# The start of a fused attention and gated-MLP block on one core: the first unit's scores by pairs of heads, and the loads and turns around them in another order

## The chip, the core and the metric

The kernel runs on one core of one Trainium2 chip. The metric is the device time of one execution in microseconds. A core has five engines with a queue each: TensorE (PE in the profile; its weight loads are shown as PEld), VectorE (DVE), ScalarE (ACT), GpSimd (POOL) and SyncE (SP, which here only issues DMAs). An engine works through its queue in order, and each instruction waits there for what it needs from others.

## What is computed

An adaLN block: six modulation vectors from `c`, grouped-query attention with 32 query heads on 8 cached key and value heads, then a gated MLP with a spatial product. Cut to what matters:

```python
mod = (silu(c) @ w_mod).reshape(1, 6, 1, 512)      # sa, ca, ga, sb, cb, gb
h = layernorm(x) * (1 + ca) + sa                   # x: 1 x 2048 x 512, bfloat16
q = (h @ wq)                                       # 32 heads of 128
k, v = repeat(k_cache, 4), repeat(v_cache, 4)      # 8 heads x 2048 x 128
p = softmax(q @ k.T * 128 ** -0.5)
x = x + ga * ((p @ v) @ wo)
h = layernorm(x) * (1 + cb) + sb
z = gelu(h @ w_in)                                 # 2 x 896
g = w_sp @ layernorm(z[..., 896:]) + b_sp          # along the sequence
x = x + gb * ((z[..., :896] * g) @ w_out)
```

## The kernel before

The 2048 rows of x are 16 tiles of 128 rows, in 4 chunks of 4 tiles. The attention works in 128 units: unit u is key/value group g = u // 16 and row tile j = u % 16, with the 4 query heads of that group. A unit has 8 slots. In a slot `qk` (L992) makes two tiles of 128 keys against the 4 heads (two matmuls of 512 columns into one of two buffers `s_ps`, L1026), and ScalarE takes the exponential of those 1024 columns into `pT` (L1033). One unit later `pv` (L1074) multiplies by v, eight matmuls of 129 columns a slot (L1082); later still `wo_proj` (L1106) adds the output projection. From unit 8 on every second unit is done by rows in another way (L1003 to L1023). The loop at L1375 writes all this out by hand, unit by unit and slot by slot: in each slot first what the table `later` holds for it (entered by `at`), then the scores, then a share of `pv`, then what the table `fill` holds, mostly the projection of q for a coming chunk (`qproj`, L935), a matmul or two a slot. Nothing reorders it: the order of the calls is the order in each engine's queue.

Before unit 0 can start, a chain has to run once, and the change is in it:

- Loads. SyncE's queue takes, in this order: the first 1024 columns of the modulation weight (`wmod_a`, two halves by columns, L707), the first group's `wq` (two halves along the contraction, L752), half of the first 8 key tiles (`k_nat`, L753), x tile 1, the other half, x tiles 2 and 3 (L756), the last 8 key tiles transposed by DMA (L760), v (L732), the rest of x (L764) and wo. ScalarE's queue takes `c` (L703) and then x tile 0 (L704).
- Modulation. VectorE and ScalarE make silu(c) (L773 to L782). `mod_part` (L853) multiplies a part of the weight by it, 16 matmuls of one column a part; `mod_copy` (L865) copies the two results to `modc`, adding 1 to the scale.
- x tile 0. VectorE takes statistics (`ln_stats`, L696), GpSimd the reciprocal root (`rstd_of`, L676), VectorE normalises (L687), TensorE transposes in four pieces (L894), and VectorE and ScalarE apply the modulation to two pieces each, which gives `hT` (L816 and L908).
- q of tile 0 for all 4 heads: 16 matmuls of 128 columns (L921) into two banks, with the turn of key tiles 0 to 3 (`k_turn`, L872) between; then VectorE and ScalarE copy a bank each (L929).
- `warm` (L784) puts matmuls on zeros into TensorE's queue, here and there, that nobody reads.

Inside unit 0, slot 0's fill `first_norm` (L1198) turns key tiles 4 to 7, and takes statistics and normalises tiles 1 to 3; `first_turn` in slot 3 turns tile 1 to hT (`ln1_turn`, L825: transposes on TensorE, modulation on VectorE), slot 6 turns tiles 2 and 3. Slots 4 and 5 project q of tile 1, slot 7 and unit 1 q of tiles 2 and 3 (`rest_q`, L1216). Chunk 1 of x is handled by `ln1_at` (L1221): its statistics stand in unit 0, slot 7, its normalisation in unit 1, slot 2, its transposes by DMA from SyncE one slot later (`ln1_dma`), its modulation (`ln1_dma_mod`) in unit 2, slot 2. Chunk 2 follows from unit 2, slot 4. GpSimd's queue loads the other 2 MB of the modulation weight in unit 2, slot 5 (`wmod_b` in the tile `wsp`, L1231); 32 matmuls on it stand in unit 4, slot 4 (`mod_cols_b`, L1171).

Of the kernel before, what the change touches and what calls it, by code (L numbers as in the profile page):

```python
# [12 lines left out]
ACT = mybir.ActivationFunctionType  # L13
ALU = mybir.AluOpType
AX = mybir.AxisListType
P = 128
# [559 lines left out]
def kernel(  # L576
# [19 lines left out]
    nc = tc.nc  # L596
# [103 lines left out]


    c_bf = res.tile([P, NDT], BF16, name="c_bf")
    nc.scalar.dma_start(out=c_bf[:], in_=c_dram)  # L703
    nc.scalar.dma_start(out=x_sb[:, 0, :], in_=x_dram[:, 0, :])  # L704
    for i in range(2):
        part = slice(i * D, (i + 1) * D)
        nc.sync.dma_start(out=wmod_a[:, :, part], in_=wmod_dram[:, :, part])  # L707
    k_nat = early.tile([P, SK], BF16, name="kT")

    def load_k_nat(half):  # L710
        t0, t1 = half * NKT // 4, (half + 1) * NKT // 4
# [85 lines left out]
    def ln1_stats(j0, n):  # L797
        for j in range(j0, j0 + n):
            ln_stats(mv1, j, x_sb[:, j, :])
        return rstd_of(mv1[:, j0 : j0 + n, :], n, "ln1")  # L800

    def ln1_norm(j0, n, rstd):
        xns = []
        for j in range(j0, j0 + n):
            xn = res.tile([P, D], BF16, name="xn1", bufs=4)
            normalise(xn[:], x_sb[:, j, :], mv1[:, j, 0:1], rstd[:, j - j0 : j - j0 + 1])
            xns.append(xn)
        return xns
# [73 lines left out]
            copy(out=kT0[:, part[0] * P : (part[-1] + 1) * P], in_=k_ps[:, 0 : n * P])  # L882


    xns0 = ln1_norm(0, 1, ln1_stats(0, 1))
    mc_ps = bank("misc")
    warm(10)
    mod_part(0, wmod_a, 0, mc_ps)
    warm(6)
    mod_part(1, wmod_a, D, mc_ps)  # L890

    x_ps = [bank("misc")[:].bitcast(BF16), bank2()[:, 0:512].bitcast(BF16)]
    for dt in range(NDT):
# [2 lines left out]
            xns0[0][:, dt * P : (dt + 1) * P],  # L896
            ident[:],
        )
    mod_copy(0, mc_ps)
    warm(2)  # L900
    hT_of(0)
    for k in range(2):
        for dt in (2 * k, 2 * k + 1):
# [9 lines left out]
                    bias=modc[:, dt : dt + 1],  # L913
                )
    qTs = {0: early.tile([P, REP, 512], BF16, name="qT")}
    q_ps = [bank("misc"), bank2()]
    for dt in range(NDT):
        if dt == 2:
            k_turn((0, 1, 2, 3), (nc.vector.tensor_copy, nc.scalar.copy))
        for hh in range(REP):  # L920
            nc.tensor.matmul(  # L921
                q_ps[hh // 2][:, hh % 2 * P : (hh % 2 + 1) * P],
                lhsT=wqs[0][:, dt, hh * DH : (hh + 1) * DH],
                rhs=hTs[0][:, dt, 0:P],
                start=(dt == 0 and hh % 2 == 0),
                stop=(dt == NDT - 1 and hh % 2 == 1),
            )
    for hf, copy in enumerate((nc.vector.tensor_copy, nc.scalar.copy)):
        copy(  # L929
            out=qTs[0][:, 2 * hf : 2 * hf + 2, 0:P],  # L930
            in_=q_ps[hf][:, 0 : 2 * P].rearrange("p (h q) -> p h q", h=2),
        )
    warm(2)

    def qproj(b, heads, c0, n, banks=("misc", "misc")):  # L935

# [55 lines left out]
    def qk(u, i):  # L992
# [10 lines left out]
        if by_rows(u):  # L1003
            hh, half = divmod(i, 2)
            for c in range(2):
                k0 = (2 * half + c) * 512
                nc.tensor.matmul(  # L1007
                    s_ps[:, c * 512 : (c + 1) * 512],
                    lhsT=qTs[b][:, hh, jj * P : (jj + 1) * P],
                    rhs=groups[g]["kT"][:, k0 : k0 + 512],  # L1010
                    start=True,
                    stop=True,
                )
            nc.scalar.activation(  # L1014
                out=rows_of(u, hh)[:, half * HK : (half + 1) * HK],
                in_=s_ps[:],
                func=ACT.Exp,
                scale=inv_sqrt_dh,
                accum_out=rsums[u][:, i : i + 1],
            )  # L1020
            if half == 1:
                at(*divmod(u * NSLOT + i + 2, NSLOT), lambda: turn_rows(u, hh))
            return  # L1023
        for h in range(2):
            kt = 2 * i + h
# [564 lines left out]
```

## Time and profile before

| | us |
|---|---|
| median of 3 runs | 1311.34 (1311.04 to 1311.53) |
| the profiled execution | 1311.72 |
| its span, first to last instruction | 1309.7 |
| TensorE busy in the span | 1301.9 (99%) |
| ScalarE busy | 1112.4 (85%) |
| VectorE busy | 684.2 (52%) |
| GpSimd busy | 58.7 (4%) |

The 2.0 us between the span and the execution lie around the span and hold no instruction of the program. Matmuls are pipelined, so a busy TensorE may be one at less than its peak.

Where the start goes (stretches of the span; busy us of each engine):

| stretch | what | TensorE | VectorE | ScalarE |
|---|---|---|---|---|
| 0 to 11.26 | to the first exponential of unit 0 | 9.80 | 4.79 | 3.04 |
| 11.26 to 18.36 | unit 0 | 6.72 | 6.21 | 6.85 |
| 18.36 to 26.75 | unit 1 | 8.39 | 6.05 | 7.91 |
| 26.75 to 48.20 | units 2 to unit 4, slot 3 | 21.45 | 11.23 | 19.23 |

A line of the timeline gives start, us, engine, line, operation, what it writes and reads, count, and in brackets the idle time of the engine before it and what ended that. An exponential of 1024 columns is 1.02 long, but the next one starts 0.91 after it.

### The profile page before, as it was taken

Reading aid. Unit: us, or ns where it says so; the run is one execution under the profiler, and the core shown is the slowest. Engines: PE = TensorE matmul, PEld = TensorE weight load, DVE = VectorE, ACT = ScalarE, POOL = GpSimd, SP = SyncE. Lnnn points to the kernel's source line nnn. Section 1 sums busy time; section 2 is a strip of 40 time slices with the busy share of each in tenths; the row PEclk is TensorE's granted clock in tenths of the full one; section 3 lists DMA queues with packets and bytes.
Section 4 is the critical chain, followed back from the end, with each engine's and each line's share of the span. In section 5 each row is a group of like instructions: output and inputs, shape, how many; then the busy total and the mean of one; then the engine's idle time right before and its main releaser. Section 6 shows DMA issues by size and latency. Waiting matters only on the chain.

```text
span 1309.7 us, 24370 instructions
## 1 busy us (share of the span) xinstructions
PE 1301.9 (99%) x9527; PEld 736.3 (56%) x9527; DVE 684.2 (52%) x1693; ACT 1112.4 (85%) x1533; POOL 58.7 (4%) x116
## 2 busy tenths in 40 slices
PE   9999999999999999999999999999999999999998
PEld 5665555555555555555555555555555555644445
DVE  6544544444445454444454544444555588784443
ACT  7899999999999999999999999999999999550000
POOL 1200000000000000000000000000000011120000
PEclk9999999999999999999999999999999999999999
DMA  7668778877887677867986678678776688464300
GB/s 181 153 94 154 129 127 159 154 126 133 153 168 143 126 139 155 145 130 137 169 160 127 125 156 156 128 137 153 163 144 124 119 141 147 105 134 96 85 21 31
DMA packets 607723, 174.45 MB, mean 133 GB/s; under 512 B 597264, under 2 KB 603664, under 8 KB 607600
## 3 DMA queue, kind: packets, MB, share of 16 engines
q1 hardware_dynamic: 600576, 153.67, 65.0%
q0 software_dynamic: 4432, 16.91, 4.2%
q10 hardware_dynamic: 2592, 2.23, 0.5%
q8 instruction: 77, 1.26, 0.4%
q14 instruction: 46, 0.38, 0.1%
HBM read 21.89 MB, written 2.10 MB: 18 GB/s over the span
## 4 chain that ended last, share of the span: by engine, by line
PE 97%; DMA 2%; DVE 1%; POOL 0%; issue 0%; ACT 0%; SPq 0%; DVEq 0%
PE o_ps L1082 18%; PE s_ps L1026 18%; PE s_ps L1007 16%; PE o_ps L1061 16%; PE misc L1114 8%; PE misc L947 8%; PE misc L1457 7%; PE s_ps L1292 2%; PE s_ps L1331 2%; PE o_ps L1490 1%; DMA wsp<-in_w_mod_dram 1%; PE s_ps L1490 0%; DMA wmod_a<-in_w_mod_dram 0%; DMA hT<-xn 0%; DVE hT L816 0%; DVE bnst L698 0%
## 5 line engine op out<-in xcount | busy, mean ns | idle before, releaser
L1033 ACT ACTIVATE pT<-s_ps 128x1024 bf16<-128x1024 f32 x552 | 560.4, 1024 | 32.1 <-PE s_ps L1026 10.1
L1082 PEld LDWEIGHTS <-pT 128*128 128x128 bf16 x4416 | 295.3, 98 | 128.9
L1082 PE MATMUL o_ps<-v,pT 128*128 128x129 bf16 x4416 | 339.7, 220 | 0.0
L1026 PE MATMUL s_ps<-qT,kT 128*128 128x512 bf16 x1104 | 328.1, 379 | 0.3 <-ACT pT L1033 0.2
L1007 PE MATMUL s_ps<-kT,qT 128*128 128x512 bf16 x944 | 280.7, 379 | 0.1
L1014 ACT ACTIVATE win_sb<-s_ps 128x1024 bf16<-128x1024 f32 x238 | 243.4, 1024 | 3.5
L1114 PE MATMUL misc<-wo_g,oT 128*128 128x512 bf16 x512 | 194.0, 379 | 0.0
L947 PE MATMUL misc<-hT,wq_g 128*128 128x512 bf16 (+2 forms) x520 | 187.0, 371 | 0.1
L1026 PEld LDWEIGHTS <-kT 128*128 128x128 bf16 x1104 | 107.2, 98 | 115.0 <-issue 2.3
L1014 ACT ACTIVATE pn<-s_ps 128x1024 bf16<-128x1024 f32 x156 | 159.4, 1023 | 2.0 <-ACT wmod_a L1014 0.3
L1061 PEld LDWEIGHTS <-v 128*128 128x128 bf16 x944 | 92.3, 98 | 111.5
L958 DVE CAST qT<-misc 128x512 bf16<-128x512 f32 x125 | 85.6, 685 | 123.5 <-PE misc L947 123.5
L1070 DVE CAST oT<-o_ps 128x512 bf16<-128x512 f32 x59 | 40.8, 691 | 195.0 <-PE o_ps L1061 195.0
L1061 PE MATMUL o_ps<-wsp,v 128*128 128x512 bf16 x480 | 142.1, 379 | 0.0
L1061 PE MATMUL o_ps<-pT,v 128*128 128x512 bf16 x464 | 138.0, 379 | 0.0
L1007 PEld LDWEIGHTS <-qT 128*128 128x128 bf16 x944 | 92.2, 98 | 61.7 <-issue 0.2
L1047 DVE TENSOR_TENSOR tot<-rs 128x1 f32<-128x1 f32 x236 | 36.1, 153 | 127.3 <-ACT win_sb L1014 84.9
L1457 PE MATMUL misc<-wsp,z 128*128 128x512 bf16 (+2 forms) x560 | 100.5, 336 | 0.0
L1052 DVE TENSOR_SCALAR win_sb<-win_sb,rall 128x2048 bf16<-128x2048 bf16 x119 | 89.6, 753 | 4.4 <-DVE rall L1050 0.3
L1014 ACT ACTIVATE wmod_a<-s_ps 128x1024 bf16<-128x1024 f32 x78 | 79.8, 1023 | 0.0
L1457 PEld LDWEIGHTS <-z 128*128 128x128 bf16 x560 | 50.5, 98 | 48.4 <-issue 0.2
L1127 DVE TENSOR_TENSOR xacc<-misc,xacc 128x512 f32<-128x512 f32 x112 | 76.0, 679 | 0.0
(111 smaller groups left out, 817.4 us busy)
## 6 DMA issues: line engine op xcount, KB each, us to landing
v<-in_A_v_cache_dram POOLq DMA_DIRECT2D x7, 512.0 KB, 6.6
wq_g<-in_A_wq_dram POOLq DMA_DIRECT2D x7, 512.0 KB, 4.9
wo_g<-in_A_wo_dram POOLq DMA_DIRECT2D x7, 512.0 KB, 4.3
wsp<-in_w_mod_dram POOLq DMA_DIRECT2D x1, 2048.0 KB, 11.8
out_dram<-yout ACTq DMA_DIRECT2D x16, 128.0 KB, 1.7
win_sb<-in_B_w_in_dram POOLq DMA_DIRECT2D x1, 1792.0 KB, 8.1
x_sb<-in_A_x_dram SPq DMA_DIRECT2D x3, 512.0 KB, 8.1
oT<-onorm SPq DMA_TRANSPOSE x69, 2.8
```

What stands on the lines that cost most here:

```text
L947: nc.tensor.matmul(ps[0][:, o0 : o0 + n], lhsT=wqs[g][:, dt, hh * DH : (hh + 1) * DH], rhs=hTs[ch][:, dt, c0 : c0 + n], start=(dt == 0), s ...
L958: nc.vector.tensor_copy(out=dst, in_=src)
L1007: nc.tensor.matmul(s_ps[:, c * 512 : (c + 1) * 512], lhsT=qTs[b][:, hh, jj * P : (jj + 1) * P], rhs=groups[g]["kT"][:, k0 : k0 + 512], sta ...
L1014: nc.scalar.activation(out=rows_of(u, hh)[:, half * HK : (half + 1) * HK], in_=s_ps[:], func=ACT.Exp, scale=inv_sqrt_dh, accum_out=rsums[u ...
L1026: nc.tensor.matmul(s_ps[:, h * 512 : (h + 1) * 512].rearrange("p (r q) -> p r q", r=REP), lhsT=groups[g]["kT"][:, kt * P : (kt + 1) * P], ...
L1033: nc.scalar.activation(out=pTs[u][:, 2 * i : 2 * i + 2, :], in_=s_ps[:].rearrange("p (k q) -> p k q", k=2), func=ACT.Exp, scale=inv_sqrt_dh,)
L1052: nc.vector.tensor_scalar(out=rows, in0=rows, scalar1=rinv, scalar2=None, op0=ALU.mult)
L1061: nc.tensor.matmul(o_pss[u][:], lhsT=groups[g]["v1"][:, kt, 0:DH], rhs=pTs[u][:, kt, :], start=(kt == 0), stop=(kt == NKT - 1),)
L1082: nc.tensor.matmul(o_ps[:, hh % 2, 0 : DH + 1], lhsT=pTs[u][:, kt, hh * P : (hh + 1) * P], rhs=groups[g]["v1"][:, kt, 0 : DH + 1], start=( ...
L1114: nc.tensor.matmul(X_ps[:], lhsT=oTs[u][:, hh, :], rhs=groups[g]["wo"][:, hh, :], start=(hh == 0), stop=(hh == REP - 1),)
L1127: nc.vector.tensor_tensor(out=xaccs[j][:], in0=X_ps[:], in1=xaccs[j][:], op=ALU.add)
L1457: nc.tensor.matmul(g_pss[f][:, :n], lhsT=z2[:, st, f * P : (f + 1) * P], rhs=wsp[t][:, st, c0 : c0 + n], start=(st == 0), stop=(st == NT - ...
```

## The change

- On ScalarE's queue x tile 0 is issued ahead of `c`.
- `wmod_a` is loaded in a piece of three quarters of the contraction and one of the last quarter, with all 1024 columns each, instead of two pieces by columns. Its matmuls go with it: `mod_first` takes one of four parts of the contraction, 8 matmuls, and accumulates all 8 columns in one bank; the 1 of the scale is added by a matmul of a constant into the same bank, so that one copy replaces `mod_copy`. Three parts run before the transposes of x tile 0, the fourth after them and one warm matmul. Six warm matmuls between the parts go, and those around the copy are placed anew.
- The first `wq` is loaded and used by pairs of heads: the first pair's columns, then half of the key tiles, then the second pair's columns. `first_q(0)` projects q for the first pair before unit 0; `first_q(1)` stands in slot 0's fill, behind the scores of slot 0. VectorE copies both. The turn of key tiles 0 to 3 stands behind `first_q(0)`.
- A slot of unit 0 makes four key tiles against two heads instead of two tiles against four: four matmuls of 256 columns. Even slots take the first pair, odd slots the second.
- The turn of tile 1 stands in slot 4 instead of 3, that of tiles 2 and 3 in slot 7 instead of 6, ahead of the statistics of chunk 1; the warm fills and the projection of tile 1 move a slot too. All 16 matmuls of `rest_q` are in unit 1, slots 1 to 6; before, 4 of them were in unit 0, slot 7, and 12 in unit 1, slots 0 to 5.

```diff
     c_bf = res.tile([P, NDT], BF16, name="c_bf")
+    nc.scalar.dma_start(out=x_sb[:, 0, :], in_=x_dram[:, 0, :])
     nc.scalar.dma_start(out=c_bf[:], in_=c_dram)
-    nc.scalar.dma_start(out=x_sb[:, 0, :], in_=x_dram[:, 0, :])
-    for i in range(2):
-        part = slice(i * D, (i + 1) * D)
-        nc.sync.dma_start(out=wmod_a[:, :, part], in_=wmod_dram[:, :, part])
+    for kts in (slice(0, NDT - 1), slice(NDT - 1, NDT)):
+        nc.sync.dma_start(out=wmod_a[:, kts, :], in_=wmod_dram[:, kts, 0 : 2 * D])
...
-    for dts in (slice(0, 2), slice(2, 4)):
-        nc.sync.dma_start(out=wqs[0][:, dts, :], in_=wq_dram[:, dts, 0 : REP * DH])
+    pairs = [slice(2 * hf * DH, 2 * (hf + 1) * DH) for hf in range(2)]
+    nc.sync.dma_start(out=wqs[0][:, :, pairs[0]], in_=wq_dram[:, :, pairs[0]])
     load_k_nat(0)
+    nc.sync.dma_start(out=wqs[0][:, :, pairs[1]], in_=wq_dram[:, :, pairs[1]])
...
+    def mod_first(kt, mc_ps):
+        for col in range(2 * NDT):
+            nc.tensor.matmul(
+                mc_ps[:, col : col + 1],
+                lhsT=wmod_a[:, kt, col * P : (col + 1) * P],
+                rhs=sc_bf[:, kt : kt + 1],
+                start=(kt == 0 and col == 0),
+                stop=(kt == NDT - 1 and col == 2 * NDT - 1),
+            )
+        if kt == 0:
+            nc.tensor.matmul(
+                mc_ps[:, NDT : 2 * NDT],
+                lhsT=mean_bf[:],
+                rhs=ones_bf[:, 0:NDT],
+                start=False,
+                stop=False,
+            )
...
     warm(10)
-    mod_part(0, wmod_a, 0, mc_ps)
-    warm(6)
-    mod_part(1, wmod_a, D, mc_ps)
+    for kt in range(NDT - 1):
+        mod_first(kt, mc_ps)
...
-    mod_copy(0, mc_ps)
-    warm(2)
+    warm(1)
+    mod_first(NDT - 1, mc_ps)
+    nc.vector.tensor_copy(out=modc[:, 0 : 2 * NDT], in_=mc_ps[:, 0 : 2 * NDT])
+    warm(4)
...
-    q_ps = [bank("misc"), bank2()]
-    for dt in range(NDT):
-        if dt == 2:
-            k_turn((0, 1, 2, 3), (nc.vector.tensor_copy, nc.scalar.copy))
-        for hh in range(REP):
...
+    def first_q(hf):
+        q_ps = bank("misc")
+        for dt in range(NDT):
+            for k in range(2):
+                hh = 2 * hf + k
+                nc.tensor.matmul(
+                    q_ps[:, k * P : (k + 1) * P],
+                    lhsT=wqs[0][:, dt, hh * DH : (hh + 1) * DH],
+                    rhs=hTs[0][:, dt, 0:P],
+                    start=(dt == 0 and k == 0),
+                    stop=(dt == NDT - 1 and k == 1),
+                )
+        nc.vector.tensor_copy(
             out=qTs[0][:, 2 * hf : 2 * hf + 2, 0:P],
...
-    warm(2)
+    first_q(0)
+    k_turn((0, 1, 2, 3), (nc.scalar.copy, nc.vector.tensor_copy))
...
-    first = dict(r1=ln1_stats(1, 1))
+    first = {}
...
+        if u == 0:
+            k0, qs = i // 2 * 4, slice(i % 2 * 256, (i % 2 + 1) * 256)
+            for kt in range(4):
+                nc.tensor.matmul(
+                    s_ps[:, kt * 256 : (kt + 1) * 256].rearrange("p (r q) -> p r q", r=2),
+                    lhsT=groups[g]["kT"][:, (k0 + kt) * P : (k0 + kt + 1) * P],
+                    rhs=qTs[b][:, i % 2 * 2 : i % 2 * 2 + 2, 0:P],
...
     def first_norm():
+        first_q(1)
+        first["r1"] = ln1_stats(1, 1)
         k_turn((4, 5, 6, 7), (nc.vector.tensor_copy,))
...
-    at(0, 3, first_turn)
-    at(0, 6, lambda: ln1_turn(2, 2, first["x2"]))
+    at(0, 4, first_turn)
+    at(0, 7, lambda: ln1_turn(2, 2, first["x2"]))
     fill[0, 0] = [first_norm]
-    for i in (1, 2, 3):
+    for i in (2, 3, 4):
         fill[0, i] = [lambda: warm(1)]
     next_q = qproj(0, list(range(REP)), P, P)
-    fill[0, 4], fill[0, 5] = next_q[0:8], next_q[8:16]
+    fill[0, 5], fill[0, 6] = next_q[0:8], next_q[8:16]
     rest_q = qproj(0, [0, 1], 2 * P, 2 * P) + qproj(0, [2, 3], 2 * P, 2 * P)
-    fill[0, 7] = rest_q[0:4]
     for i in range(6):
-        fill[1, i] = rest_q[4 + 2 * i : 6 + 2 * i]
+        fill[1, i + 1] = rest_q[(8 * i + 2) // 3 : (8 * i + 10) // 3]
```

More of the change, by code (lines that the diff above doesn't have):

```diff
@@ L915 @@
     qTs = {0: early.tile([P, REP, 512], BF16, name="qT")}
-    q_ps = [bank("misc"), bank2()]
-    for dt in range(NDT):
-        if dt == 2:
-            k_turn((0, 1, 2, 3), (nc.vector.tensor_copy, nc.scalar.copy))
-        for hh in range(REP):
[L921 to L929, printed above, removed]
+    def first_q(hf):
[11 more added lines that the diff above has]
+        nc.vector.tensor_copy(
             out=qTs[0][:, 2 * hf : 2 * hf + 2, 0:P],
-            in_=q_ps[hf][:, 0 : 2 * P].rearrange("p (h q) -> p h q", h=2),
+            in_=q_ps[:, 0 : 2 * P].rearrange("p (h q) -> p h q", h=2),
         )
-    warm(2)
+    first_q(0)
+    k_turn((0, 1, 2, 3), (nc.scalar.copy, nc.vector.tensor_copy))
     def qproj(b, heads, c0, n, banks=("misc", "misc")):
@@ L1022, in qk @@
                 at(*divmod(u * NSLOT + i + 2, NSLOT), lambda: turn_rows(u, hh))
+            return
+        if u == 0:
[5 more added lines that the diff above has]
+                    rhs=qTs[b][:, i % 2 * 2 : i % 2 * 2 + 2, 0:P],
+                    start=(kt % 2 == 0),
+                    stop=(kt % 2 == 1),
+                )
+            nc.scalar.activation(
+                out=pTs[u][:, k0 : k0 + 4, qs],
+                in_=s_ps[:].rearrange("p (k q) -> p k q", k=4),
+                func=ACT.Exp,
+                scale=inv_sqrt_dh,
+            )
             return
```

## The prediction

> **What bounds the kernel now.** I read the page's first two parts (TensorE is busy 99% of the span, in every slice but the last), then all waits of TensorE, because an engine that is never idle can only be delayed where it waits. There are four in the whole execution (engine, line, what it waited for, total us, times, longest):
>
> ```profile
> PE o_ps L788 <- DVE onorm L769: 1.2, 1, 1.2
> PE misc L857 <- DMA wsp<-in_w_mod_dram: 0.7, 1, 0.7
> PE s_ps L1026 <- ACT pT L1033: 0.2, 1, 0.2
> PE misc L857 <- DMA wmod_a<-in_w_mod_dram: 0.2, 1, 0.2
> ```
>
> Three lie in the first 13 us, which the change rewrites. The second lies behind them, at 48.2 to 48.9 us: TensorE stands 0.69 us for the large part of the modulation weight (it is loaded into the tile wsp). After it TensorE never waits again, so the end moves exactly as far as that point moves. The chain of waits, in order of time (start, us, what), tells what sets it:
>
> ```profile
> 16.93 1.28 DVE hT L816 x4
> 27.29 3.10 DMA hT<-xn
> 30.52 1.38 DVE hT L816 x4
> 36.04 1.00 POOL rstd_ln L683
> 37.04 11.81 DMA wsp<-in_w_mod_dram
> 48.90 0.95 PE misc L857 x32
> ```
>
> The load leaves GpSimd's queue at 37.04, behind the rstd of chunk 2 (L683), which needs chunk 2's statistics, which stand in VectorE's queue behind the modulation of chunk 1 (30.52), which waits for the transposes of chunk 1, which follow its normalisation. The timeline of VectorE shows where that begins:
>
> ```profile
> 16.23 0.69 DVE L958 CAST qT<-misc 128x512 bf16<-128x512 f32 x1 [0.51 <-PE misc L947]
> 16.84 0.72 DVE L816 TENSOR_SCALAR hT<-misc,modc 128x256 bf16<-128x256 bf16 x2
> 17.48 0.72 DVE L816 TENSOR_SCALAR hT<-o_ps,modc 128x256 bf16<-128x256 bf16 x2
> 18.12 0.68 DVE L698 BATCH_NORM_STATS2 bnst<-x_sb 128x6 f32<-128x512 bf16 x1
> ...
> 22.89 1.38 DVE L687 TENSOR_SCALAR xn<-x_sb,mv,rstd_ln 128x512 bf16<-128x512 bf16 x4 [0.91 <-POOL rstd_ln L683]
> ```
>
> No gap stands between 16.23 and the end of chunk 1's statistics: they start at 18.12 because the turn of tiles 2 and 3 (L816, 16.84) is ahead of them. So two clocks run: VectorE's, which lands the load 30.73 us after 18.12, and TensorE's, which arrives at 48.21. The load is the later by 0.69.
>
> **The change, step by step.** Times are those of the profiled execution (span 1309.7, execution 1311.72). M is the start of the modulation's last matmuls, H that of the first hT modulation (8.36 before), S that of unit 0's fourth exponential (13.98 before).
>
> 1. *c behind x tile 0.* Before, c was issued at 0.73, had its first packet at 1.72 and landed at 2.47; x tile 0, second on the queue at 1.14, had its first packet at 2.97 and released VectorE at 4.74. Now c is second. Bounds: 2.95 (its old landing plus the 0.45 that x's issue takes) and 4.70 (x's own landing, though c is 1 KB). I take 3.7: x's first packet, the nearest row, plus the 0.75 from c's first packet to its landing. VectorE waits for c first (L773), and the statistics of x tile 0 are queued behind that wait; x being earlier brings them nothing. The silu was partly hidden: L773 ended at 2.67 and ACT's exponential began only at 2.91, after its table load. Without that, L773 to the statistics is 0.22 + 0.94 (2.91 to 3.85) = 1.16. Statistics at 3.75 + 1.16 = 4.91, xn done 2.34 later (4.74 to 7.08 before): 7.25.
>
> 2. *Weight split along the contraction.* 24 of 32 matmuls and the added 4-column one run after the first transfer, beside nothing else: free. Packets of 2 KB for 1 KB cost, per KB, between 46 ns (1 KB rows) and 40 ns (4 KB rows at 162 ns), so the last part lands between 7.0 and 7.39. But TensorE keeps order: four transposes that wait for xn now stand ahead of the last eight matmuls. M = 7.25 + 0.04 + 0.22 (four at 55 ns) + 0.22 (one warm) = 7.73, against 7.43 before. Eight matmuls (0.19 + 0.16) and one copy instead of 16 and two: H = M + 0.63 instead of M + 0.92. **H = 8.36, as before.** By the bounds of c: 7.95 (the weight then decides) to 9.35.
>
> 3. *Pairs.* The last of eight matmuls of the first pair starts at H + 0.91 (the fourth hT is out at H + 0.81), ends H + 1.12; cast 0.42 (row of 10.10) to H + 1.58; VectorE's k copy, 0.29, now behind that cast, to H + 1.79; four 256-column scores at 109 ns, and the first exponential starts at **H + 2.38**, against H + 2.90. Here the change gains 0.5. The second pair gives it back: its projection is behind slot 0's scores on TensorE (eight at 56 ns from H + 2.19, done H + 2.80), then the cast to H + 3.26, then slot 1's scores to H + 3.91: second exponential at H + 3.95, 1.57 after the first, where the old ones followed each other by 0.91. Slot 2 needs k tiles 4 to 7, whose copy is in VectorE's queue behind that cast and the statistics of x tile 1 (0.68 + 0.18): copied at H + 4.42, third exponential H + 5.11, fourth H + 6.02 (before: H + 5.63). So S = 14.38, **0.39 later**. The wq halves by pairs have runs of 512 B, between 965 packets/us (256 B rows) and 343 (1 KB rows): 0.75 to 1.06 us each, the first there by 8.5 at the latest and needed at 8.76; hidden. Doubled weight loads (98 ns beside 109 ns) are hidden too.
>
> 4. *Turns one slot later.* Before, chunk 1's statistics started S + 4.14. Now the turn of tiles 2 and 3 stands in slot 7: scores of slot 6 at S + 2.00 (end of the fifth exponential), eight projections, eight transposes, cast at S + 3.08, and the old 1.89 from cast to statistics: S + 4.97. So 0.83 later, and with step 3 **1.22 later**: statistics 19.34, load issued 38.26, landed 50.07.
>
> 5. *TensorE's own clock.* Unit 1 starts at S + 3.79 = 18.17 (18.36 before), but carries four more 256-column projections, 0.44. Their two casts are now behind chunk 1's four normalisations in VectorE's queue (24.11 to 25.5); unit 2 needs the second: 27.30 against 26.75, so TensorE arrives at 48.76, still before the load.
>
> **Sum:** 0 (steps 1, 2) + 0.39 + 0.83 = 1.22, all of it seen at the wait for wsp, which grows from 0.69 to 1.3: execution 1311.72 + 1.2 = 1312.9. The median of the runs lies 0.38 under the profiled execution; on it, 1311.34 + 1.2 = **1312.5**. Dropping warm matmuls and one modulation copy is inside these figures.
>
> **Rivals.**
> *A: c later still.* x tile 0's first packet came 0.76 after the weight's first (2.20), which is 16 packets of 46 ns on one engine: a turn of the other queue. With 2 KB packets such a turn is 1.3 to 1.5 long, so c would land 0.6 later: H 8.95, end +1.8, **1313.1**. Against it: c may be in before the weight starts. [...]
>
> *B: the load stops being the gate.* From 43.94 to 46.34 most DMA engines hold one packet of it for 2.4 us while hT's transposes run beside it. If the new timing misses that hold, it lands at 47.7, TensorE's arrival decides, 48.76 against 48.90: **1311.2**, not slower. For it: transposes elsewhere in the trace hold engines 1.2 to 1.6 only. Against: the transposes shift with the load, both behind the same statistics.
>
> *C: TensorE's clock falls back, clearly slower.* The first ten warm matmuls take 0.43 each, those from 5.82 on 0.22; after the change nothing fills 5.4 to 6.3 and little does until 7.7. At half speed, steps 2 and 3 would pay 0.4 + 0.4 + 0.2 + 0.9 for 16 projections, k transposes and two slots of scores, 1.9 more: **1314.4**. It decides if the slow pitch of 0.43 is back at H. Against: the pitch changed after 3.9 us of work, and the hole is shorter. [...]
>
> *D: the pairs do what they could.* If the second exponential followed at the old pitch, S = H + 5.10 and the end +0.3, **1311.6**. The order of TensorE's instructions speaks against it.
>
> **How the numbers follow.** Forecast 0.52, A 0.15, B 0.23, C 0.05, D 0.05. The range 1310.8 to 1313.5 takes in B with an early c (0.4 less), D, A and nearly the late bound of c (+2.2). A measurement of this kernel can tell about 0.2%, 2.6 us, from no change; only C and the tail of A pass it upward, 0.07; downward I know no mechanism, 0.02 for what I overlook; 0.91 within.
>
> **What would show it.** Right: L773 near 3.75, first hT modulation near 8.4, first exponentials near 10.7, 12.3 and 13.5, chunk 1's statistics near 19.3, wsp issued near 38.3 and a wait of over 1 us for it. Step 1 is wrong if VectorE's statistics of x tile 0 start well off 4.9; step 3 if the second exponential follows the first within 1.1; step 4 if statistics start under 18.6; the whole if TensorE no longer waits for wsp.

## The result, and the profile after

The changed kernel takes 1320.44 us (median of 6 runs, 1318.61 to 1324.10) beside 1311.43 for the kernel before (6 runs, 1311.04 to 1312.45): a ratio of 1.0070, 95% interval 1.0056 to 1.0084. It is 9.0 us slower. The forecast was 1312.5 and the range ended at 1313.5. Two rivals pointed further this way, A (c later still, 1313.1) and C (TensorE's clock, 1314.4), and each was far too small.

All waits of TensorE in the profiled execution after (1321.69 us, span 1319.7; engine, line, what it waited for, total us, times, longest):

```profile
PE s_ps L1028 <- ACT win_sb L1035: 2.4, 1, 2.4
PE misc L887 <- DVE sc_bf L782: 1.5, 1, 1.5
PE misc L911 <- DVE xn L687: 1.4, 1, 1.4
PE misc L1496 <- DVE gb L1523: 1.2, 1, 1.2
PE o_ps L788 <- DVE onorm L769: 1.2, 1, 1.2
PE s_ps L1048 <- DVE kT L882: 0.5, 1, 0.5
PE s_ps L1048 <- DVE qT L948: 0.3, 1, 0.3
PE s_ps L1048 <- ACT kT L882: 0.3, 1, 0.3
```

The wait for wsp, which the whole forecast hung on, is gone from the list. Four new long waits stand in it: for the silu of c (L782), for the first normalised tile (L687), and two far behind the lines that the change touches. Of the three short ones (L1048) the two on VectorE are those between the scores of the pairs, which step 3 of the prediction counted. VectorE's timeline after shows where the first two begin:

```profile
5.89 0.17 DVE L773 CAST c_f<-c_bf 128x4 f32<-128x4 bf16 x1 [4.63 <-DMA c_bf<-in_c_dram]
...
6.94 0.17 DVE L782 CAST sc_bf<-sc 128x4 bf16<-128x4 f32 x1
7.02 0.69 DVE L698 BATCH_NORM_STATS2 bnst<-x_sb 128x6 f32<-128x512 bf16 x1
7.74 0.18 DVE L699 BATCH_NORM_AGGREGATE mv<-bnst 128x2 f32<-128x6 f32 x1
8.94 0.41 DVE L687 TENSOR_SCALAR xn<-x_sb,mv,rstd_ln 128x512 bf16<-128x512 bf16 x1 [1.02 <-POOL rstd_ln L683]
```

c, 1 KB, released VectorE at 5.89 and not at 3.75. From there on the steps are as long as forecast: 1.13 to the statistics (1.16), 1.92 more to the start of xn and 2.33 to its end (2.34). TensorE's timeline over the same time:

```profile
1.18 4.45 PE L788 MATMUL o_ps<-onorm 128*128 128x512 bf16 x10 [1.18 <-DVE onorm L769]
7.17 0.35 PE L887 MATMUL misc<-sc_bf,wmod_a 128*128 128x1 bf16 x8 [1.54 <-DVE sc_bf L782]
...
9.41 0.29 PE L911 MATMUL misc<-ident,xn 128*128 128x128 bf16 x1 [1.44 <-DVE xn L687]
9.49 0.31 PE L911 MATMUL s_ps<-ident,xn 128*128 128x128 bf16 x1
9.60 0.31 PE L911 MATMUL misc<-ident,xn 128*128 128x128 bf16 x1
9.71 0.31 PE L911 MATMUL s_ps<-ident,xn 128*128 128x128 bf16 x1
9.81 0.63 PE L788 MATMUL o_ps<-onorm 128*128 128x512 bf16 x1
...
10.50 1.87 PE L788 MATMUL o_ps<-onorm 128*128 128x512 bf16 x4
12.16 1.06 PE L941 MATMUL misc<-hT,wq_g 128*128 128x128 bf16 x8
```

The last number in brackets is idle time and its releaser: TensorE stood from 5.63 to 7.17 and from 7.97 to 9.41. The pitch tells the clock: transposes start 0.11 apart (0.055 before), the warm matmuls start 0.43 apart (0.22 before, from 5.82 on). In the trace the clock rises to full at 13.49; before, it did at 5.06. The first exponential starts at 14.55 (11.26 before), the first matmul on wsp at 52.51 (48.90).

So of the 8.88 us by which TensorE's last matmul ends later (1313.34 against 1304.46), 3.61 are there by 52 us. The rest comes in two places that no line of the diff touches: 2.42 at 88.6 us with the clock at half (granted clock 0.50) from 92.00 to 95.41 behind it (half of 3.41 is 1.7), and 1.20 at 1197. The sum is 8.9. Another 1.1 lies behind the last matmul. The 3.6 of the start are two halves: e8 below, with c as late but the full clock, reaches the matmuls on wsp at 50.62, 1.7 behind the kernel before, and the changed kernel is 1.9 behind e8.

### The profile page after: what moved, and what is told of

It reads as the page before. It is cut to its first block, busy times and chain, and to the rows that moved or that the text cites. A ratio compares the mean times of both kernels' runs of the same rounds, so it can differ in the third digit from the quotient of the medians.

```text
span 1319.7 us, 24391 instructions
## 1 busy us (share of the span) xinstructions
PE 1304.2 (99%) x9539; PEld 739.6 (56%) x9539; DVE 685.2 (52%) x1693; ACT 1113.1 (84%) x1532; POOL 59.1 (4%) x116
## 4 chain that ended last, share of the span: by engine, by line
PE 95%; DVE 2%; DMA 1%; POOL 0%; ACT 0%; another core or an unknown queue 0%; issue 0%; ACTq 0%; DVEq 0%; POOLq 0%
PE o_ps L1120 19%; PE s_ps L1064 18%; PE s_ps L1028 16%; PE o_ps L1099 15%; PE misc L1152 8%; PE misc L968 8%; PE misc L1496 7%; PE s_ps L1331 1%; PE o_ps L1529 1%; DVE stz L1353 1%; DMA xnT<-xn 1%; PE s_ps L1529 0%; DVE z L687 0%; DMA c_bf<-in_c_dram 0%; ACT pT L1055 0%; PE s_ps L1048 0%
## 5 line engine op out<-in xcount | busy, mean ns | idle before, releaser
L1071 ACT ACTIVATE pT<-s_ps 128x1024 bf16<-128x1024 f32 x544 | 553.7, 1025 | 29.8 <-PE s_ps L1064 8.3
L1064 PE MATMUL s_ps<-qT,kT 128*128 128x512 bf16 x1088 | 323.6, 379 | 0.1
L1035 ACT ACTIVATE pn<-s_ps 128x1024 bf16<-128x1024 f32 x156 | 159.6, 1024 | 2.0 <-ACT pn L1035 0.3
L1496 PE MATMUL misc<-wsp,z 128*128 128x512 bf16 (+2 forms) x560 | 100.5, 336 | 1.2 <-DVE gb L1523 1.2
L1035 ACT ACTIVATE wmod_a<-s_ps 128x1024 bf16<-128x1024 f32 x78 | 79.9, 1024 | 0.4 <-ACT wmod_a L1035 0.3
L1496 PEld LDWEIGHTS <-z 128*128 128x128 bf16 x560 | 50.5, 98 | 49.7 <-issue 1.5
```

The lines of the kernel that those rows point to most:

```text
L1035: nc.scalar.activation(out=rows_of(u, hh)[:, half * HK : (half + 1) * HK], in_=s_ps[:], func=ACT.Exp, scale=inv_sqrt_dh, accum_out=rsums[u ...
L1064: nc.tensor.matmul(s_ps[:, h * 512 : (h + 1) * 512].rearrange("p (r q) -> p r q", r=REP), lhsT=groups[g]["kT"][:, kt * P : (kt + 1) * P], ...
L1071: nc.scalar.activation(out=pTs[u][:, 2 * i : 2 * i + 2, :], in_=s_ps[:].rearrange("p (k q) -> p k q", k=2), func=ACT.Exp, scale=inv_sqrt_dh,)
L1496: nc.tensor.matmul(g_pss[f][:, :n], lhsT=z2[:, st, f * P : (f + 1) * P], rhs=wsp[t][:, st, c0 : c0 + n], start=(st == 0), stop=(st == NT - ...
```

## The experiments

This table gives the steps of the start (us, from each kernel's profiled execution) and the times of all of them; the kernel before had medians of 1310.97 (beside e1 to e4), 1311.03 (e5 to e8), 1310.75 (e9 to e12) and 1311.41 (e13, e14).

| kernel | cast of c | stats of x 0 | first hT | first exp | first matmul on wsp | median | ratio to before, 95% |
|---|---|---|---|---|---|---|---|
| before | 2.50 | 4.74 | 8.36 | 11.26 | 48.90 | above | |
| changed | 5.89 | 7.02 | 10.88 | 14.55 | 52.51 | 1320.44 | 1.0070 (1.0056 to 1.0084) |
| e1 | 3.46 | 5.78 | 9.64 | 12.89 | 50.86 | 1316.35 | 1.0046 (1.0032 to 1.0060) |
| e2 | 4.82 | 5.96 | 8.73 | 11.49 | 49.10 | 1311.90 | 1.0005 (0.9996 to 1.0014) |
| e3 | 2.49 | 4.76 | 8.42 | 10.77 | 48.73 | 1312.16 | 1.0007 (0.9998 to 1.0016) |
| e4 | 5.77 | 6.91 | 10.33 | 12.68 | 50.65 | 1316.90 | 1.0045 (1.0031 to 1.0059) |
| e5 | 3.65 | 5.92 | 9.35 | 11.71 | 49.67 | 1315.00 | 1.0027 (1.0018 to 1.0037) |
| e6 | 4.39 | 5.53 | 8.95 | 11.31 | 49.27 | 1315.56 | 1.0034 (1.0022 to 1.0046) |
| e7 | 5.79 | 6.92 | 10.78 | 14.45 | 52.41 | 1319.54 | 1.0063 (1.0050 to 1.0077) |
| e8 | 5.75 | 6.88 | 10.30 | 12.65 | 50.62 | 1315.95 | 1.0039 (1.0026 to 1.0053) |
| e9 | 5.71 | 6.84 | 10.27 | 14.31 | 52.27 | 1316.00 | 1.0040 (1.0027 to 1.0054) |
| e10 | 2.51 | 4.77 | 8.32 | 10.67 | 48.63 | 1311.42 | 1.0005 (0.9996 to 1.0014) |
| e11 | 3.39 | 4.66 | 8.87 | 11.22 | 49.19 | 1311.68 | 1.0005 (0.9996 to 1.0014) |
| e12 | 3.18 | 4.31 | 8.43 | 10.78 | 48.75 | 1312.84 | 1.0015 (1.0006 to 1.0024) |
| e13 | 5.90 | 7.03 | 10.89 | 14.25 | 52.21 | 1319.58 | 1.0062 (1.0049 to 1.0076) |
| e14 | 5.99 | 7.12 | 10.98 | 15.07 | 53.35 | 1318.89 | 1.0062 (1.0048 to 1.0075) |

The first theory was "late c": the start is slow because c stands behind a transfer, and the rest follows. Its rival was "missing filler": TensorE has nothing to do for so long that its clock stays at half. e1 to e4 take the change apart.

**e1, c first again.**

```diff
-    nc.scalar.dma_start(out=x_sb[:, 0, :], in_=x_dram[:, 0, :])
     nc.scalar.dma_start(out=c_bf[:], in_=c_dram)
+    nc.scalar.dma_start(out=x_sb[:, 0, :], in_=x_dram[:, 0, :])
```

> The changed kernel with the two issues of ScalarE's queue in their old order (c, then x tile 0); all else as changed. Theory 'late c': the whole loss of the start is c's. Then the cast of c starts near 2.5, the first hT modulation near 8.0 to 8.4 (10.88 in the changed kernel), the first exponential near 10.7 (14.55), TensorE's clock is full from about 5 to 6, and chunk 1's statistics start near 19.3 (23.11). If the two later losses (+4.0 near 87 us, +1.3 near 1190) follow from the late start, the execution takes 1312 to 1313; if they belong to the new turns or to the pairs, about 1316 to 1318. Rival 'missing filler': the clock stays at half until 9 or later although c is early, because nothing fills TensorE between 5.6 and its transposes; then the first exponential comes near 11.5 to 12 and the execution is 1314 or more.

Neither theory alone. c is 0.96 later than before although it is first, x tile 0 is 1.04 later, and TensorE stands 1.94 for xn. Its clock was full at 4.37, fell to half at 7.78 and came back at 11.20: a third pattern. Of the 9.0 us over the kernel before, 3.6 are gone and 5.4 stay.

**e2, the order of the two issues alone**, on the kernel before: the same two lines swapped the other way.

> The kernel before with only the order of ScalarE's two issues changed (x tile 0, then c). Theory 'late c': c waits for the share of the modulation weight that stands in each DMA engine ahead of it; here that is 16 packets of 1 KB (0.74 us at 46 ns) and not 24 of 2 KB (2.0 us at 85 ns), so the cast of c starts between 3.7 and 4.7, the first hT modulation at 9.0 to 10, and the execution takes 1312 to 1314. If c comes near 5.9 here too, the size of the weight's packets and shares has nothing to do with it, and the loss is about that of the changed kernel's start, 1314 to 1315. If the later stall near 87 us follows from any delay of the start, it is seen here too, and then 1316 to 1319. Rival 'missing filler': six warm matmuls more are here, so the clock is full from about 5 and less is lost than 2 us.

The cast of c starts at 4.82, just past the upper bound of 4.70. But the first hT is only 0.37 later, since six more warm matmuls and the second half of the weight cover it. Alone, this part costs 0.9 us, inside what the measurement can tell.

**e3, pairs and turns alone**: the changed kernel with the start of the kernel before (the two issues, the two loads of the weight by columns, the modulation by columns, six and two warm matmuls).

> Unit 0 in pairs, the queries' weight by pairs and the turns one slot later, on the start of the kernel before (c first, modulation weight by columns, six and two warm matmuls). This is steps 3 and 4 of the prediction alone. By them: first exponential 2.4 after the first hT modulation, the second 1.57 after the first, the fourth 6.0 after it, chunk 1's statistics near 19.3 and a wait for the large modulation weight of 1 us or more: 1312.6. If these steps are what brings the later losses (near 87 and 1190 us), about 1316 to 1318 with a start that is no more than 1.3 late. If the wait is gone as in the changed kernel, 1311.5 to 1312.

This is steps 3 and 4 of the prediction by themselves, and they hold to 0.1 us. ScalarE's timeline of e3:

```profile
8.42 0.80 ACT L927 ACTIVATE hT<-s_ps,modc 128x128 bf16<-128x128 bf16 x2 [5.29 <-DVE modc L869]
9.70 0.37 ACT L883 COPY kT<-o_ps 128x256 bf16<-128x256 bf16 x1 [0.47 <-PE o_ps L880]
10.77 1.02 ACT L1055 ACTIVATE pT<-s_ps 128x1024 bf16<-128x1024 f32 x1 [0.70 <-PE s_ps L1048]
12.33 5.83 ACT L1055 ACTIVATE pT<-s_ps 128x1024 bf16<-128x1024 f32 x6 [0.54 <-PE s_ps L1048]
```

From the first hT modulation (8.43 on VectorE) to the exponentials: 2.34, 3.90, 5.04 and 5.96, forecast 2.38, 3.95, 5.11 and 6.02. Chunk 1's statistics start at 19.34, to the hundredth as forecast. TensorE arrives at wsp at 48.73 (forecast 48.76), but the load is in at 48.17: it was issued at 38.60 (38.26) and took 9.57 us, not 11.81. That is rival B: the 2.4 us for which most DMA engines each held one packet of it (43.9 to 46.3 before) are not in the trace of e3; its longest packet takes 1.34. e2, without the new turns, has the hold again (2.33 at 44.2). e3 is therefore 0.17 ahead at 48.7 us. It loses 0.62 near 1190, at L1496, and ends 1.2 above the kernel before by medians, which the measurement cannot tell from nothing.

**e4, more filler at the start.**

```diff
-    warm(10)
+    warm(17)
```

> The changed kernel with 17 warm matmuls at its start for 10 (c still late), so that TensorE has work until about 6.8 and not until 5.6. Theory 'late c': the first hT modulation stays near 10.7 to 10.9 and nearly all the loss of the start stays. Rival 'missing filler' (the clock is what costs): the clock goes full near 5 as in the kernel before, the pitch of the first eight projections is about 0.06 and not 0.12, the first exponential comes 0.8 to 1.3 earlier than 14.55 and chunk 1's statistics 1 to 2 earlier than 23.11. Both agree that it stays slower than the kernel before; by 'late c' 1319 to 1321, by 'missing filler' 1317 to 1319. The stall near 87 us is watched: if it goes without the start being repaired, it hangs on the moment or on chance and not on c.

c is as late as in the changed kernel, but the clock is full from 6.85; the first exponential comes 1.87 earlier and 3.1 of the 9.0 us come back. "Missing filler" said 1317 to 1319 and "late c" 1319 to 1321; 1316.90 is just under both. So e1 takes back 3.6 us by an earlier c, and e4 3.1 with c still late. Both act on one chain, whose parts in the changed kernel are: c late (5.89), TensorE idle (1.54 and 1.44), clock low (to 13.49).

**e5, c first and filler behind the first three contraction tiles**: e1 with `warm(8)` after the loop over `mod_first`.

> The kernel with c first of the first group of runs (1316.35), and eight warm matmuls more behind the first three contraction tiles of the modulation, where TensorE stood 1.94 us and its clock then fell to half from 7.78 to 11.20. Theory 'hole': that fall is most of what this kernel has over the one with pairs and turns alone (1312.16). Then the clock stays full from its first rise on, the first exponential comes 0.8 to 1.3 before 12.89, and the execution takes 1313.5 to 1315. Rival 'transfers': the modulation weight in larger packets makes x tile 0 land 1 us late (5.78 for 4.76), and that is the loss; then the fall of the clock goes and the execution stays within 1 us of 1316.35.

The clock is full from 5.64 to the end. The first exponential comes 1.18 earlier than in e1, inside the 0.8 to 1.3 of "hole", and the execution is 1.4 nearer to the kernel before than e1's, at the upper edge of what "hole" said. x tile 0 is late as in e1 (5.92); 4.0 us stay.

**e6, the modulation weight in four loads.**

```diff
-    for kts in (slice(0, NDT - 1), slice(NDT - 1, NDT)):
+    for kts in (slice(kt, kt + 1) for kt in range(NDT)):
```

> The changed kernel with the first 1 MB of modulation weight in four loads of one contraction tile (8 packets of 2 KB on an engine each) for two loads (24 and 8). c is still second on ScalarE's queue. Theory 'share': c waits on every engine until the transfer that began before it is through, 24 packets of 85 ns; with 8 packets, 0.7 us, its cast starts near 4.0 to 4.4 (5.89 in the changed kernel), the first hT modulation 1 to 1.5 earlier than 10.88, and the execution gains 1 to 4 on the changed kernel's 1320. Rival 'turn of some number of packets whatever the transfer': 16 packets of 85 ns, the cast near 5; rival 'all of the queue': nothing changes, 5.9.

The cast of c starts at 4.39: "share" said 4.0 to 4.4. The first hT comes 1.93 earlier (1 to 1.5 expected), and 4.5 of the 9.0 us are gone. The packets show how long c waits. Counting the weight's packets that had started, per DMA engine, when the middle packet of the second transfer on ScalarE's queue ran: 24.7 in the changed kernel, 24.6 in e7, 24.1 in e4, 23.9 in e1 and 23.8 in e5, where the first load has 24 on an engine; 8.1 in e6 and 8.4 in e11, where it has 8. In these kernels the middle packet of the second transfer ran as the first load ended. It is 16.5 before, 16.3 in e3 and 19.1 in e2, and there the first load is 512 rows of 1 KB, 32 on each of 16 engines: the second transfer came about half way through it, not behind it as the 16 in the expectation of e2 has it. So neither the whole load nor a fixed number of packets fits all of them, and the rule behind it stays open. The 16 of before, which the prediction took for a turn of the queues, were half of a load. Shown is that the wait grew to 24 packets of 85 ns, 2.0 us, and that with loads of 8 packets c came 1.50 earlier (4.39 for 5.89).

**e7, the changed kernel once more.** No edit.

> The changed kernel itself, once more, for the stall at 88.6 us (2.42 us of TensorE, with the clock at half for 3.41 us behind it) and for the spread of its runs. If the stall belongs to the kernel, it is in this profile too, at unit 8's first score groups, and the execution is near 1321. If it is chance of one execution, it is gone, and the profiled execution is near 1317.5 (1321.7 less 2.4 and 1.7); what is left over the kernel before is then the start (3.6), the wait near 1190 (about 1) and the end.

The start is the same (full clock at 13.59) and the stall is there again, shorter: TensorE stood 1.36 at 88.54. The execution, 1319.46, lies between the two expectations. Beside ScalarE's timeline of the first profile:

```profile
86.42 1.02 ACT L1035 ACTIVATE win_sb<-s_ps 128x1024 bf16<-128x1024 f32 x1
87.35 0.19 ACT L1035 ACTIVATION_READ_ACCUMULATOR win_sb<-s_ps 128x1 f32 x1
89.89 1.02 ACT L1035 ACTIVATE win_sb<-s_ps 128x1024 bf16<-128x1024 f32 x1 [2.35 <-remote]
```

and of e7:

```profile
86.33 1.02 ACT L1035 ACTIVATE win_sb<-s_ps 128x1024 bf16<-128x1024 f32 x1
87.25 0.19 ACT L1035 ACTIVATION_READ_ACCUMULATOR win_sb<-s_ps 128x1 f32 x1
88.73 1.02 ACT L1035 ACTIVATE win_sb<-s_ps 128x1024 bf16<-128x1024 f32 x1 [1.29 <-PE s_ps L1028]
```

The second exponential of unit 8 starts 2.35 and 1.29 late, in both for the release by the scores' matmul. That matmul's record ends at 87.27 and 87.18; its semaphore moves at 89.87 and 88.71. This is the same place twice, so not the accident of one execution; e13 and e14 below show how much it varies. A shorter late release stands in the kernel before too: the scores' matmul ends at 70.68, and ScalarE is released at 71.18. TensorE has other work there and does not stand. So such a release does not take a slow start. In e7 no fall of the clock follows (two score matmuls take 0.60 at 92.00), and 1.67 are lost at L1496.

**e8, no hole in the start**: the changed kernel with `warm(17)` and `warm(4)` behind the loop over `mod_first`.

> The changed kernel with 17 warm matmuls at its start for 10 and four more behind the first three contraction tiles of the modulation, so that TensorE does not stand over 0.5 us before the first scores; c is still late. Theory 'hole': with 17 alone it stood 0.89 us and its runs went from 1314.6 to 1317.8; if those are runs in which the clock fell, they are gone here, and the runs lie near 1314 to 1315 with a spread under 1.5. Rival 'late c' alone: the median stays near 1316.9. If the spread stays, something else than the clock makes it.

No wait of TensorE over 0.5 us between its first matmul and the first scores, full clock from 6.69, no stall at 88; but 1315.57 to 1317.16, over the 1314 to 1315 of "hole". Its profile shows 0.7 near 1190 and 1.6 us more behind the last matmul than before. The spread fell from 3.2 us in e4 to 1.6, near the 1.5 of "hole", but at a level above it. That e4's slower runs were those in which the clock fell is not borne out.

**e9, as late as the changed kernel, with the full clock**: e8 with `warm(12)` for the `warm(4)` ahead of the first hT.

> The kernel without the hole (17 and 4 warm matmuls, c late, 1315.95) with eight more warm matmuls (8 times 0.22) ahead of the first hT projections: unit 1 starts about 3.5 us later than in the kernel before, as in the changed kernel, but TensorE has its full clock. It is for the stall at 87 to 90 us, which both profiles of the changed kernel have (2.42 and 1.36 us) and no other kernel's. Theory 'moment': the stall comes from how late the start is against the transfers of that time; then it is here too, 1 to 3 us at unit 8's second or third score group. Rival 'clock': it goes with the slow start itself, whatever the lateness; then it is gone, and the profiled execution is 1.8 above that of the kernel without the hole.

This is the cleanest pair of the study. e9's first matmul on wsp is at 52.27, the changed kernel's at 52.51; the clock of e9 is full from 3.86. No stall, at the same place of the program:

```profile
86.19 1.02 ACT L1036 ACTIVATE win_sb<-s_ps 128x1024 bf16<-128x1024 f32 x1
87.11 0.19 ACT L1036 ACTIVATION_READ_ACCUMULATOR win_sb<-s_ps 128x1 f32 x1
87.20 1.02 ACT L1036 ACTIVATE win_sb<-s_ps 128x1024 bf16<-128x1024 f32 x1
```

Its five runs lie between 1315.92 and 1317.10. So "moment" is not borne out: being 3.4 us late costs 5.2 us by medians and brings no stall. The four kernels with the slow start (changed, e7, e13, e14) are 7.5 to 9.0 above before, 2.2 to 3.8 more than e9. How much of that comes behind 52 us differs: in the profiled executions TensorE loses 5.3 there in the changed kernel, 3.4 in e7, 2.2 in e13 and nothing in e14 or e9, while e14 reaches wsp 1.1 later than e9. "Clock" had e9's profiled execution 1.8 above e8's; it is 0.2 above, because e8 loses 0.8 near 1190 and 0.7 behind the last matmul that e9 does not.

**e10, pairs and turns alone, with the range check later**: e3 with the five instructions that test the softmax sums moved behind the fifth gate of the spatial projection (the fourth, as the expectation counts them; the trace has five gates ahead of the check).

```diff
         for f in range(NFT):
             spatial(t, yTs[t], f, 0, 512)
+            if t == 0 and f == CT:
+                bad = range_check()
```

> Pairs and turns alone (1312.16), with the range check of the softmax sums (five instructions of VectorE, 2.3 us, which stand ahead of the first gate of the spatial projection) moved behind the fourth gate. Nothing is left out. Theory: at 48 us that kernel is 0.18 ahead of the kernel before, and loses 0.62 again near 1190, where TensorE waits for that gate. Without the check ahead of it the wait is gone and the lead stays: 1311.3 to 1311.7, no different from the kernel before by this measurement. Rival: VectorE is late there by more than the check, and a wait stays: 1312.

The wait at the gate is gone, and 1311.42 cannot be told from the kernel before. But the lead does not stay, as the theory had it: TensorE of the profiled execution is 0.36 ahead up to 1187 and 0.26 behind from 1189 on. Three matmuls (L1498, from 1187.88) start 0.43 apart in place of 0.22, each just behind one of VectorE's last normalisations of z (L687, released at 1187.84, 1188.26 and 1188.68). VectorE is late there without the check too; the list of waits does not show it, since the gaps between the records are only 0.02 to 0.04 long.

**e11 and e12, the changed kernel repaired.** e11: c first, four loads, `warm(12)` and `warm(4)` around the first three contraction tiles, the range check later. e12 the same, with c on SyncE's queue ahead of the weight:

```diff
-    nc.scalar.dma_start(out=c_bf[:], in_=c_dram)
+    nc.sync.dma_start(out=c_bf[:], in_=c_dram)
```

> The changed kernel repaired: c first again, the modulation weight in four loads of one contraction tile, 12 warm matmuls at the start and four behind the first three contraction tiles, and the range check later. Theory 'share': x tile 0 waits for no more than 8 packets of 2 KB on an engine and lands by 4.3 to 4.6, c by 2.6; statistics at 4.4, the first hT modulation at 7.8 to 8.1 (8.36 before), the first exponential near 10.3, TensorE at its full clock from its first rise, about 0.6 ahead of the kernel before at 50 us, no wait near 1190: 1310.5 to 1311.3. Rival 'transfers still in the way': x lands near 5 and the hole costs a fall of the clock: 1313 or more.

> As the repaired kernel, but c is issued on SyncE's queue ahead of the modulation weight, so that x tile 0 is first on ScalarE's queue and c does not stand behind it. Theory 'order on a queue': both are early: the cast of c at 2.5 to 2.7, the statistics of x tile 0 near 3.9 (right behind the silu), the weight 0.4 to 0.5 later than with c on ScalarE's queue; the last part of the weight, near 7.3, then sets the first hT modulation, 8.0 to 8.4, no better than the repaired kernel: 1310.8 to 1311.6. Rival: the two queues take turns so that c or x waits for the weight anyway, and the first hT modulation is after 8.6: 1312 or more.

x tile 0 came 0.3 later than expected in e11 (statistics at 4.66, expected 4.4), c 0.8 later (3.39, expected 2.6), and the first hT missed (8.87, not 7.8 to 8.1). Here the filler was in the way: the clock rose only at 7.03, twelve warm matmuls at half speed lasted to 6.28, and TensorE reached the transposes at 7.85, 0.85 after xn was out. All the same 8 of the 9 us are gone. In e12 c (3.18, expected 2.5 to 2.7) and the statistics (4.31, expected 3.9) came late as well; the first hT (8.43) was 0.03 past its range, and TensorE is 0.15 ahead at 48.7 us. Its execution is 1312.84 and not 1310.8 to 1311.6. Its profile shows no wait of TensorE that explains this and 0.8 more behind the last matmul than before or e11. No version beats the kernel before; e2, e3, e10 and e11 cannot be told from it.

**e13, the modulation's rows earlier, and e14, the changed kernel with the range check later** (as e10's edit).

```diff
-    at(5, 4, mod_rows)
+    at(5, 1, mod_rows)
```

> The changed kernel with the modulation's row parts (two matmul groups, GpSimd's writes and the broadcast loads of ga_rows and gb_rows) three slots earlier in unit 5. Theory 'transfer': in both profiles of the changed kernel the broadcast load of gb_rows is issued at 86.8 and 88.7, behind the first scores of unit 8, and in the other kernels' at 82.8 to 84.8, ahead of them; TensorE's release of ScalarE comes 1.5 and 2.6 us late just then. With the load about 3 us earlier the stall is gone, and the execution is 1316 to 1317.5. Rival 'slow start': the stall hangs on something else that the slow start brings; it stays, with 1319 to 1321.

> The changed kernel with the range check behind the fourth gate of the spatial projection, as in the kernel with pairs and turns alone. Theory: the wait near 1190 (1.20 and 1.67 us in two profiles) is VectorE's lateness behind transposes that land late; without the 2.3 us of the check it is gone, and the execution is 1318 to 1319, 1.2 to 1.7 under the changed kernel's. Rival: VectorE is later than the check is long, and the gain is under 0.5. A third profile of the changed kernel's first 1,100 us comes with it: by 'slow start' the stall near 88 us is there again; by chance it need not be.

e13's transfer is issued at 85.50, only 1.3 earlier than in e7 and not 3; its stall is 0.3, but its median is as before the edit. And e14, where that transfer is issued at 86.72 (86.77 in e7), has no stall at all. So "transfer" isn't borne out. With the start as slow in all four, the stall was 2.4, 1.4, 0.3 and 0. e14's wait at L1496 is gone; this is VectorE's timeline near it in the changed kernel, with the check ahead of the gate:

```profile
1174.69 0.98 DVE L1196 TENSOR_SCALAR hT<-xnT,modc 128x128 bf16<-128x128 bf16 x4 [5.21 <-DMA xnT<-xn]
...
1196.26 0.69 DVE L1474 TENSOR_TENSOR tmp<-tmp 128x512 f32<-128x512 f32 x1
1196.98 0.69 DVE L1476 TENSOR_REDUCE okm<-tmp 128x1 f32<-128x512 f32 x1
1197.70 0.16 DVE L1478 TENSOR_SCALAR bad<-okm 128x1 bf16<-128x1 f32 x1
1197.78 0.69 DVE L1523 TENSOR_TENSOR gb<-misc,bsp_bc 128x512 bf16<-128x512 f32 x1
```

and in e14:

```profile
1172.05 0.98 DVE L1196 TENSOR_SCALAR hT<-xnT,modc 128x128 bf16<-128x128 bf16 x4 [5.73 <-DMA xnT<-xn]
...
1191.13 1.78 DVE L687 TENSOR_SCALAR z<-z,mvz,rstd_lnz 128x896 bf16<-128x896 bf16 x4 [1.48 <-POOL rstd_lnz L683]
1193.39 0.69 DVE L1525 TENSOR_TENSOR gb<-misc,bsp_bc 128x512 bf16<-128x512 f32 x1 [0.48 <-PE misc L1498]
```

In the first the gate (L1523) follows the check with no gap and TensorE waits for it; in the second VectorE itself waits 0.48 for TensorE. What makes VectorE late is the first line of each: it stands over 5 us for the last transposed tile (3.24 before, at 1165.12). Over the kernel before, e14 is 7.5 and the changed kernel 9.0 and 8.5, a gain of 1.0 to 1.5 (1.2 to 1.7 were expected); with runs of e14 from 1317.16 to 1322.14 its size is not resolved.

## Why the prediction was wrong

**Step 1 failed, at its bound.** "4.70 (x's own landing, though c is 1 KB)" was taken as the latest that c could come; it came at 5.89. The row it came from, x tile 0 second on its queue, was behind 16 packets of 46 ns. In the changed kernel c is behind 24 packets of 85 ns, 2.0 us, and step 2 did count the larger packets, but only as a cost of the load itself. From c's first packet (4.67) to VectorE's release it took 1.2 more, where step 1 had 0.75. e6 shows that smaller loads bring c earlier (4.39), e2 what the old loads give (4.82).

**Rival A was right that c waits behind the weight's packets, with a wrong size.** It priced a turn at 16 packets (1.3 to 1.5) and c at 0.6 later; the runs show no fixed turn of 16 (16.5 packets before, 24.7 here, 8.1 in e6), and c was 2.1 later than the forecast's 3.75.

**The rest of steps 1 and 2 holds from there**: 5.77 + 1.16 + 2.34 + 0.48 + 0.63 gives a first hT at 10.38 for e4, which has the full clock; 10.33 was measured. In the changed kernel it was 10.88: the half clock added the rest.

**Rival C was given 0.05 and 1.9 us, and it came true beside A, not in its place.** Its price was right for the start: the changed kernel is 1.9 behind e8 at the matmuls on wsp. "Against: the pitch changed after 3.9 us of work, and the hole is shorter" looked at the hole that the dropped warm matmuls leave when c is on time. With c late there are two, 1.54 and 1.44. The prediction weighed its rivals one at a time, though A opens the hole that C needs. In the profiled execution the half clock acts before 13.49 and between 92.00 and 95.41. In the start A and C together make 3.6 of the 9 us; e8, which has the full clock throughout, still takes 4.9 more than the kernel before.

**Steps 3 and 4 were right to 0.1 us** up to chunk 1's statistics, as e3 shows (the load was issued 0.34 later than forecast), and step 5's arrival of TensorE too (48.73 for 48.76). Rival D falls with them: the second exponential of e3 starts 1.56 after the first. That the load would still end last was wrong: rival B held. With the new turns the load took 9.3 to 9.6 us (changed, e3, e5, e6), and no profile with them has a wait for it.

**"After it TensorE never waits again, so the end moves exactly as far as that point moves"** was wrong in the first section already. It was read from one execution, in which VectorE came to the first gate at 1188.90 after 0.79 of idle time. Where the last transposed tile near 1165 lands later, that margin is used up and TensorE waits 0.6 to 1.7 (e3, e6, e8, e1, e13, e7 and the changed kernel; no wait in e4, e5 and e9).

Still open: what holds the release at 87 us in two of four slow-started profiles; why e1, e4, e5, e6, e13 and e14 have medians 1.0 to 2.9 above their profiled executions; and the 0.8 to 1.6 us behind the last matmul in some kernels.

## What to carry to other kernels

A small transfer that others wait for goes ahead on its queue (the cast of c at 3.46 in e1, at 5.89 in the changed kernel); behind another, its price has to be counted in the packets of the changed kernel's loads (here 24 of 85 ns), and a turn read from the old loads does not bound it. When an input that TensorE's first work waits for is moved later, the holes it opens are to be redrawn with the new time before the clock is judged. "Never waits again" is a statement about margins: look up how long each engine was idle before every later hand-over, not only whether TensorE waited.

## What the runs showed of the hardware

The clock changes stood 3.41 us apart or twice that: 7.78 to 11.20 (e1), 92.00 to 95.41 (changed), 9.25 to 12.67 (e13), 8.75 to 15.57 (e14). Counted in stretches of 3.41 from a change, TensorE idle for 1.93 lost the full clock (e1, 4.37 to 7.78), for 1.46 kept it (e6, 6.12 to 9.53), and at half it was not given the full one with 1.03 of idle time (changed, 3.25 to 6.66, counted back from 13.49). In kernels that kept TensorE busy until then, the first rise came anywhere from 3.86 (e9) to 7.03 (e11), and the start of the changed kernel, run four times, had the full clock only from 13.49 and 13.59 on (changed, e7) or for one stretch from 5.84 and 5.33 on (e13, e14). So the same start was given the full clock at different times from one execution to the next. In these stretches 1.46 of 3.41 idle (43%) did not lose the clock and 1.93 (57%) did; nothing between the two was measured.

A slow start does not show in the row of the granted clock. These are stretches of the changed kernel (from and to; length, TensorE's busy time and instructions; granted clock; DMA share; GB/s):

```profile
0.00:4.00 4.00, 2.82 (x7) 1.00 0.54 137
8.00:12.00 4.00, 2.59 (x17) 1.00 1.25 243
92.00:96.00 4.00, 4.00 (x25) 0.57 0.74 140
```

The third has the fall of 92.00 to 95.41 in it. The first two read 1.00 although equal warm matmuls took 0.43 in them and 0.22 later: the trace has no record of the clock ahead of its first change, here 13.49. There the clock is read from the pitch of equal matmuls.
